# Fixing the order of all engines by a list schedule in the kernel, with a narrower chunk mask

## The chip, the cores and the metric

The kernel runs on one core of one Trainium2 chip. The metric is the time of one execution on the device in microseconds (us), median of several runs; lower is better. The core has five engines that run side by side, each through its own list of instructions in order: TensorE (PE in the profile, with weight loads shown apart as PEld), VectorE (DVE), ScalarE (ACT), GpSimd (POOL) and SyncE (SP, which here only issues DMAs). They meet through semaphores.

## The reference

Two layers follow each other. The first is attention in which every query may look only at six chunks of 32 keys. The second is an MLP with a spatial gate.

```python
# q, k, v: (B=4, H=8, S=768, D=64);  chunk = 32, 24 chunks, top_k = 6
k_min, k_max = min and max of k over each chunk                   # per dimension
ub = sum_d max(q*k_min, q*k_max)                                  # (B, H, S, 24)
ub = where(chunk of query >= chunk, ub, -1e9)
top_chunks = argsort(ub)[-6:]
scores = q @ k.T / 8, masked to the chosen chunks and to key <= query
attn = softmax(scores);  x = attn @ v                             # -> (B, S, 512)

h = relu(x @ w_in)                                                # (B, S, 1024)
u, v = h[..., :512], h[..., 512:]
v_n = (v - mean(v)) / sqrt(var(v) + 1e-6)
v_s = w_spatial @ v_n + b_spatial                                 # over the sequence
out = (u * v_s) @ w_out                                           # (B, S, 512)
```

## The kernel before

The 32 heads are worked on as 16 pairs of heads, `i = 0..15`; four pairs make one batch `b`. For each pair, k and q are transposed; the minimum and maximum of k per chunk (`kmm`) are reduced on VectorE and laid out as the operand `km`; relu(q) and relu(-q) (`rq`) times `km` give the bounds `ub`; VectorE takes the eight largest of each row and marks the chunks under the sixth. The marks are written beside q, transposed with it to the operand `a`, and the score matmul adds the penalty through the operand `kh` (k with the constant `expand` in its other half). ScalarE takes the exponential, TensorE multiplies by v, VectorE normalises, and `xT` is the transposed result. When the four pairs of a batch are done, its MLP runs: groups v, u, s, o of six tiles each.

```python
TILES = [[(0, 0, 512, 0)], [(1, 128, 512, 0)], [(2, 256, 512, 0)],      # score tiles of one head
         [(3, 384, 384, 0), (1, 640, 128, 384)], [(4, 512, 256, 0), (0, 512, 256, 256)], [(5, 640, 128, 0)]]
ps_sc = ...psum_pool(bufs=3); ps_tr = ...(bufs=1); ps_acc = ...(bufs=1); ps_ml = ...(bufs=3)

def init_masks():
    nc.gpsimd.memset(later, 0.0)                       # later: [128, 5 * 2 * 24 = 240]
    nc.gpsimd.affine_select(out=lv, in_=lv, compare_op=Alu.is_ge, fill=NEG, base=CPT,
                            channel_multiplier=1, pattern=[[CPT, NQT - 1], [0, 2], [-1, NCH]])
    # ... cut: tri, the causal mask within a tile
# --- in class Pair ---
def k_transpose(self):                                 # six PE transposes into a ps_ml tile
    for t in range(NQT):
        nc.tensor.transpose(kT[:, t * P:(t + 1) * P], self.k[:, t], identity)
def k_max(self): nc.vector.tensor_reduce(self.kmm[:, 0, :], ...kT..., op=Alu.max)
def k_min(self): nc.vector.tensor_reduce(self.kmm[:, 1, :], ...kT..., op=Alu.min, negate=True)
def k_operand(self, hi):
    copy = nc.scalar.copy if self.i < 1 else nc.vector.tensor_copy
    copy(self.kh[hi][d0:d1], self.kT[d0:d1])
def bounds(self):
    ub = self.ub = ps_tr.tile([P, 512], F32, tag="tr", name="ub")
    mm(ub[:, 0:(NQT - 1) * W], lhsT=sub_chunk, rhs=later, start=True, stop=False)        # 240 columns
    for qi in range(1, NQT):
        for m in range(2):
            mm(ub[:, (qi - 1) * W:qi * W], lhsT=self.rq[:, m, qi * P:(qi + 1) * P], rhs=self.km[:, m]..., ...)
def a_copy(self, hi):                                  # pairs 0..7; pairs 8..15 by a DMA transpose
    copy = nc.vector.tensor_copy if self.i < 2 and hi == 0 else nc.scalar.copy
    copy(self.a[:, :, hi, :], self.tr...)
def scores(self, hi, g):                               # matmul and exponential are one step
    sc = ps_sc.tile([P, 512], F32, tag="sc", name="sc")
    # ... cut: one or two matmuls, for batch 0 the causal mask by one more
    nc.scalar.activation(out=self.e[hi][...], in_=sc[:, 0:width], func=Act.Exp, scale=scale)
# ... cut: values, normalise, x_transpose
# --- the order: a table of beats, twelve to a pair ---
for i, p in enumerate(pairs):
    t0 = i * BEATS
    for hi in range(2):
        for g in range(len(TILES)):
            at(t0 + 6 * hi + g, p.scores, hi, g)
        at(t0 + 6 * hi + 6, p.values, hi, LOWER[0], True)
        # ... cut
first, count = (b + 1) * HP * BEATS + 13, HP * BEATS   # beats of the MLP of batch b
for cost, fn in steps:
    at(first + done * count // total, fn)
# ... cut: start-up steps by hand
with tc.manual_schedule(engines={mybir.EngineType.PE}):
    for beat in sorted(b for b in beats if b < 6):
        for fn, args in beats.pop(beat):
            fn(*args)
for beat in sorted(beats):
    for fn, args in beats[beat]:
        fn(*args)
```

Only TensorE's order up to beat 6 is fixed by hand; all else goes to the framework's scheduler in the order of the beats. A step may hold instructions of several engines.

Of the kernel before, what the change touches and what calls it, by code (L numbers as in the profile page):

```python
# [10 lines left out]
F32 = mybir.dt.float32  # L11
# [5 lines left out]
P = 128  # L17
# [29 lines left out]

@with_exitstack
def kernel(
# [12 lines left out]
    B, H, S, D = q.shape  # L62
# [4 lines left out]
    NQT = S // P  # L67
    NDO = DM // P
    KO = DH // P
    HP = H // 2  # L70
    NPAIR = B * HP
    CPT = P // CHUNK
    scale = 1.0 / math.sqrt(D)
    mm = nc.tensor.matmul

# [4 lines left out]
    ps_sc = ctx.enter_context(tc.psum_pool(name="ps_sc", bufs=3))  # L80
    ps_tr = ctx.enter_context(tc.psum_pool(name="ps_tr", bufs=1))
    ps_acc = ctx.enter_context(tc.psum_pool(name="ps_acc", bufs=1))
    ps_ml = ctx.enter_context(tc.psum_pool(name="ps_ml", bufs=3))

    def ml_tile():
        return ps_ml.tile([P, 512], F32, tag="mlp", name="mlp")
# [3 lines left out]

    BEATS = 12
    beats = defaultdict(list)

    def at(beat, fn, *args):
        beats[beat].append((fn, args))

    HALF = ((0, D), (D, 2 * D))


    NB = 4
    v_ring = [ring.tile([P, 4, NQT, D + 2], F16, name=f"vt{i}") for i in range(3)]
    qs_ring = [ring.tile([P, 2, NQT, 4, D], F16, name=f"qs{i}") for i in range(3)]
# [5 lines left out]
    later = cp.tile([P, (NQT - 1) * 2 * NCH], F16)  # L110
    expand = cp.tile([D, S], F16)
    eps_t = cp.tile([P, 1], F32)

    def init_identity():
        nc.vector.memset(identity, 0.0)
        nc.gpsimd.affine_select(out=identity, in_=identity, compare_op=Alu.not_equal, fill=1.0,
                                base=0, channel_multiplier=1, pattern=[[-1, P]])

    def init_ring(i):

        nc.vector.memset(qs_ring[i][:, :, :, 0:4:3, :], 0.0)

    def init_small():
        nc.vector.memset(km_ring[0], 0.0)
        nc.vector.memset(km_ring[1], 0.0)
        nc.vector.memset(eps_t, 1e-6)
        for t in v_ring:
            nc.vector.memset(t[:, :, :, D:D + 2], 1.0)

    def init_expand():  # L130

# [5 lines left out]

    def init_masks():

        nc.gpsimd.memset(later, 0.0)  # L140
        lv = later.rearrange("p (t h c) -> p t h c", h=2, c=NCH)
        nc.gpsimd.affine_select(out=lv, in_=lv, compare_op=Alu.is_ge, fill=NEG, base=CPT,
                                channel_multiplier=1, pattern=[[CPT, NQT - 1], [0, 2], [-1, NCH]])
# [4 lines left out]
    def init_kh(i):  # L148
        for hi, (d0, d1) in enumerate(HALF):
            nc.scalar.copy(kh_ring[i][hi][d0:d1, :], expand)  # L150


    W = 2 * NCH
    xT = {}
    tiles = {}

    class Pair:
        def __init__(self, i):
            self.i = i
            self.b, self.hp = divmod(i, HP)  # L160
            self.heads = [4 * (self.hp // 2) + self.hp % 2 + 2 * hi for hi in range(2)]
            self.qs = qs_ring[i // 2 % 3][:, i % 2]
            self.kh, self.km = kh_ring[i % NB], km_ring[i % 2]
            self.e = {}

        def k_transpose(self):
            if self.i < 16:
                self.kT = kT = ps_ml.tile([P, S], F16, tag="mlp", name="kTp")
                for t in range(NQT):
                    nc.tensor.transpose(kT[:, t * P:(t + 1) * P], self.k[:, t], identity)  # L170
            else:
                self.kT = sb.tile([P, S], F16, tag="kT", name="kT", bufs=3)
                nc.sync.dma_start_transpose(out=self.kT.rearrange("d (t s) -> d t s", s=P),
                                            in_=self.k.rearrange("p t h d -> p (t h d)"))

        def k_max(self):
            self.kmm = sb.tile([P, 2, NCH], F16, tag="kmm", name="kmm")
            nc.vector.tensor_reduce(self.kmm[:, 0, :], self.kT.rearrange("d (c ch) -> d c ch", ch=CHUNK),  # L178
                                    axis=AX.X, op=Alu.max)

        def k_min(self):
# [71 lines left out]
        def a_copy(self, hi):  # L253
            if self.i >= 8:
                return
# [339 lines left out]
```

The softmax here doesn't subtract the row's maximum and nothing guards it: scores larger than these inputs give would overflow.

## Time and profile before

| | |
|---|---|
| time, median of 3 runs | 208.62 us (208.17 to 208.92) |
| span of the profiled execution | 206.9 us |
| exponentials (L271, ScalarE) | 192, 96.9 us busy |
| score matmuls (L266) | 256 |
| MLP matmuls (L388) | 432 |
| product with v (L289) | 672 |
| mask matmuls (L219), 240 columns | 16 |
| software DMA queue | 12.20 MB, 89.8% of 16 engines' span |

L numbers are lines of the kernel. The busy time of an engine is the time in which an instruction of it was running; matmuls are pipelined and their ends are modelled, so a TensorE that looks busy may still have gaps between the starts of its matmuls. The chain of waits is the work that ended last, followed back from the last instruction to whatever released it. In the timeline a row is a run of like instructions of one engine: start, length, engine, line, operation, and in brackets the idle time before it with what ended it.

### The profile page before, as it was taken

The page shows a single profiled execution, that of the slowest core. Times are in us where ns is not written, and L with a number is a line of the kernel's source. Part 1 is how long each engine was busy: PE and PEld are TensorE (multiplying, and loading weights), DVE is VectorE, ACT ScalarE, POOL GpSimd, SP SyncE. Part 2 cuts the span into 40 slices and gives each one's busy share as a digit, 9 for nine tenths or more (in the row PEclk, how much of TensorE's full clock was granted, in tenths as well). Part 3 has the DMA queues.
Part 4 walks back from the last instruction along what each step waited for, and adds up shares of the span by engine and source line. Part 5 has one row for each costly group of instructions (what it writes and reads, how often), then busy time and mean ns, then how long its engine had stood idle before and what let it go on. Part 6 is the DMA issues. An engine that isn't in the chain of part 4 may idle for free.

```text
span 206.9 us, 5068 instructions
## 1 busy us (share of the span) xinstructions
PE 187.8 (91%) x1922; PEld 115.1 (56%) x1922; DVE 154.5 (75%) x454; ACT 158.1 (76%) x326; POOL 80.5 (39%) x100
## 2 busy tenths in 40 slices
PE   0368999898899999999999999999999999999992
PEld 0266776775666665656655656565555454444440
DVE  6467979989799989899797999887647456365520
ACT  4797989899998889785989996669999830666042
POOL 7997659596992463236114111111111110000000
PEclk9999999999999999999999999999999999999999
DMA  5999999999999999979998926648782124540356
GB/s 38 92 118 154 140 178 158 173 177 167 177 162 162 97 119 128 135 130 147 149 278 153 180 62 57 127 88 158 181 166 65 38 29 92 187 152 3 72 128 256
DMA packets 114424, 27.27 MB, mean 132 GB/s; under 512 B 109536, under 2 KB 110816, under 8 KB 114400
## 3 DMA queue, kind: packets, MB, share of 16 engines
q0 software_dynamic: 76544, 12.20, 89.8%
q1 hardware_dynamic: 37856, 14.75, 36.4%
q8 instruction: 15, 0.25, 0.5%
q14 instruction: 9, 0.07, 0.1%
HBM read 24.38 MB, written 6.29 MB: 148 GB/s over the span
## 4 chain that ended last, share of the span: by engine, by line
PE 69%; ACT 17%; DVE 8%; issue 2%; DMA 2%; POOL 0%; DVEq 0%; ACTq 0%; POOLq 0%
PE mlp L388 40%; PE sc L266 12%; ACT e L271 10%; PE acc L289 7%; PE kTp L170 2%; ACT a L257 2%; DVE kmm L178 2%; PE ub L222 2%; DMA k<-in_k_dram 2%; PE trm L251 2%; ACT vraw L398 1%; PE tr L205 1%; DVE vn L412 1%; DVE kmm L182 1%; ACT u L420 1%
## 5 line engine op out<-in xcount | busy, mean ns | idle before, releaser
L271 ACT ACTIVATE e<-sc 128x512 f16<-128x512 f32 x192 | 96.9, 553 | 14.8 <-PE sc L266 13.4
L266 PE MATMUL sc<-a,kh 128*128 128x512 f16 (+3 forms) x256 | 65.5, 308 | 2.1 <-ACT e L271 1.5
L388 PE MATMUL mlp<-w_in_sb,xT 128*128 128x512 f16 x192 | 53.0, 379 | 0.1
L278 POOL TENSOR_SCALAR_AFFINE_SELECT e<-e 128x768 f16<-128x768 f16 x24 | 20.9, 869 | 66.3 <-ACT e L271 66.3
L289 PEld LDWEIGHTS <-e 128*128 128x128 f16 x672 | 31.4, 97 | 17.0 <-DVE x L297 3.8
L388 PE MATMUL mlp<-vn,wsT 128*128 128x512 f16 x144 | 37.3, 379 | 0.0
L289 PE MATMUL acc<-vt,e 128*128 128x65 f16 x672 | 35.3, 193 | 0.7 <-DVE x L297 0.4
L266 PEld LDWEIGHTS <-kh 128*128 128x128 f16 x256 | 22.7, 98 | 13.3 <-issue 0.8
L437 ACT COPY o<-mlp 128x512 f32<-128x512 f32 x24 | 14.1, 586 | 19.5 <-PE mlp L388 19.1
L400 DVE BATCH_NORM_STATS2 stats<-vraw 128x6 f32<-128x512 f32 x24 | 16.6, 693 | 12.9 <-ACT vraw L398 12.5
L388 PE MATMUL mlp<-w_out_sb,gT 128*128 128x512 f16 x96 | 25.1, 379 | 0.0
L388 PEld LDWEIGHTS <-xT 128*128 128x128 f16 x192 | 17.2, 97 | 12.6 <-issue 0.4
L427 DVE SCALAR_TENSOR_TENSOR g<-mlp,b_col,u 128x512 f16<-128x512 f32 x24 | 17.9, 748 | 7.3 <-PE mlp L388 6.2
L232 DVE MAX8 max<-ub 128x8 f32<-128x8 f32 (+4 forms) x160 | 15.6, 165 | 5.1 <-PE ub L222 4.9
L388 PEld LDWEIGHTS <-wsT 128*128 128x128 f16 x144 | 12.9, 98 | 10.4
L178 DVE TENSOR_REDUCE kmm<-kTp 128x24 f16<-128x768 f16 x16 | 15.2, 948 | 3.7 <-PE kTp L170 2.7
L297 DVE TENSOR_TENSOR x<-acc,rec 128x384 f16<-128x384 f32 x32 | 17.6, 551 | 0.4
L336 POOL DMA_DIRECT2D qs<-in_q_dram x14 | 14.6, 1049 | 5.9 <-PE sc L266 5.9
L194 DVE COPY kh<-kTp 64x768 f16<-64x768 f16 x30 | 16.5, 549 | 0.5
L398 ACT ACTIVATE vraw<-mlp 128x512 f32<-128x512 f32 x24 | 14.4, 601 | 3.0 <-PE mlp L388 3.0
L420 ACT ACTIVATE u<-mlp 128x512 f16<-128x512 f32 x24 | 14.3, 598 | 1.7 <-PE mlp L388 1.5
L327 POOL DMA_DIRECT2D k<-in_k_dram x14 | 14.4, 1045 | 2.5 <-PE kTp L170 1.8
(67 smaller groups left out, 230.2 us busy)
## 6 DMA issues: line engine op xcount, KB each, us to landing
out_dram<-o SPq DMA_DIRECT2D x24, 256.0 KB, 2.3
vt<-in_v_dram POOLq DMA_DIRECT2D x8, 384.0 KB, 8.8
k<-in_k_dram POOLq DMA_DIRECT2D x14, 192.0 KB, 8.1
qs<-in_q_dram POOLq DMA_DIRECT2D x14, 192.0 KB, 7.5
ws_raw<-in_moe_w_spatial_dram POOLq DMA_DIRECT2D x6, 192.0 KB, 6.9
w_in_sb<-in_moe_w_in_dram POOLq DMA_DIRECT2D x8, 128.0 KB, 6.9
w_out_sb<-in_moe_w_out_dram POOLq DMA_DIRECT2D x4, 128.0 KB, 7.9
k<-in_k_dram POOLq DMA_DIRECT2D x4, 96.0 KB, 3.4
```

What stands on the lines that cost most here:

```text
L178: nc.vector.tensor_reduce(self.kmm[:, 0, :], self.kT.rearrange("d (c ch) -> d c ch", ch=CHUNK), axis=AX.X, op=Alu.max)
L194: copy(self.kh[hi][d0:d1], self.kT[d0:d1])
L266: mm(sc[:, col:col + n], lhsT=self.kh[hi][:, t * P:(t + 1) * P], rhs=self.a[:, q0 // P:(q0 + n) // P, hi, :], start=True, stop=not diag)
L271: nc.scalar.activation(out=self.e[hi][:, g * 512:g * 512 + width], in_=sc[:, 0:width], func=Act.Exp, scale=scale)
L278: nc.gpsimd.affine_select(out=blk, in_=blk, compare_op=Alu.is_ge, fill=0.0, base=0, channel_multiplier=-1, pattern=[[0, NQT], [1, P]])
L289: mm(self.av[:, qi, :], lhsT=self.e[hi][:, c:c + P], rhs=self.v[hi][:, t, 0:D + 1], start=first and n == 0, stop=last and n == len(blocks) ...
L297: nc.vector.tensor_tensor(self.x16[:, :, hi, :], in0=self.av[:, :, 0:D], in1=rec.to_broadcast([P, NQT, D]), op=Alu.mult)
L388: mm(st[group][:, 0:cols], lhsT=lhsT, rhs=rhs, start=(j == 0), stop=(j == n - 1))
L398: nc.scalar.activation(st["vraw"][:, ti, :], h, func=Act.Relu)
L400: nc.vector.bn_stats(stats, st["vraw"][:, ti, :])
L420: nc.scalar.activation(st["u"][:, ti, :], h, func=Act.Relu)
L427: nc.vector.scalar_tensor_tensor(g, in0=vs, scalar=b_col[:, ti:ti + 1], in1=st["u"][:, ti, :], op0=Alu.add, op1=Alu.mult)
```

## The change

The kernel brings its own scheduler. It describes every step as work of a single engine (matmul and exponential, for instance, become two steps), with a duration, the steps it depends on, the buffers it takes and frees, and a priority that is much like the beat it had. It plays these through once while the program is built, always starting the step that can start earliest and, among steps within 0.02 us, the one with the smallest priority. The kernel then emits the steps in that order, and the order holds on every engine. The aim is that no engine waits for a step that the framework's own estimates put at the wrong place. The dependencies in the model are those of data and of buffers.

The second part is the mask: for the bounds of a query tile only the four chunks of the tile itself need one, since the later ones are never looked at. So `later` shrinks to 5 x 2 x 4 = 40 columns, written by one matmul into the columns of each tile's own chunks. `PLAN` also lets the MLP of a batch begin 8 rather than 13 beats after its last pair's beats.

```diff
+def lat(a,b):
+    if a==b: return {'PE':0.0,'ACT':0.0,'DVE':0.0,'POOL':0.0,'SP':0.0}.get(a,0)
+    if b=='PE': return 0.055 if a!='DMA' else 0.135
+    if b in('ACT','DVE'): return 0.037 if a!='DMA' else 0.1
 # ... cut
+class Sim:
 # ... cut
+                tm=min(t for t,_ in lst)
+                t,o=min(((t,o) for t,o in lst if t<=tm+0.02),key=lambda x:(x[1].prio,x[1].idx))
+                if best is None or t<best[0]: best=(t,o)
 # ... cut
+            op(f'kT{i}','PE',6*mmc(128),PEL,deps=lk+['id1'],acq=[('ml',f'k{i}')],uses=[('k',g)],prio=pr(0)); kr=('ml',f'k{i}')
+        op(f'kmax{i}','DVE',km,.08,deps=[f'kT{i}'],acq=[('kmm',i)],uses=[kr],prio=pr(1))
+        op(f'kmin{i}','DVE',km,.08,deps=[f'kT{i}'],uses=[kr,('kmm',i)],prio=pr(2))
+            op(f'kop{i}{hi}',ke,(.70 if ke=='ACT' else .46) if not kd else .22,.1,deps=[f'kT{i}'],acq=[('kh',i)],uses=[kr],prio=pr((3 if hi==0 else 8)))
 # ... cut: all other steps
+                op(f'ex{i}{hi}{gg}','ACT',.493 if gg<5 else .16,.104,deps=[f'sc{i}{hi}{gg}'],acq=[('e',f'{i}{hi}')],uses=[('sc',f'{i}{hi}{gg}')],prio=t0+6*hi+gg+.1)
 # ... cut
+PLAN = {'late': 40, 'mlp_first': 8}
-    later = cp.tile([P, (NQT - 1) * 2 * NCH], F16)
+    later = cp.tile([P, (NQT - 1) * 2 * CPT], F16)
-        nc.gpsimd.affine_select(out=lv, in_=lv, compare_op=Alu.is_ge, fill=NEG, base=CPT,
-                                channel_multiplier=1, pattern=[[CPT, NQT - 1], [0, 2], [-1, NCH]])
+        nc.gpsimd.affine_select(out=lv, in_=lv, compare_op=Alu.is_ge, fill=NEG, base=0,
+                                channel_multiplier=1, pattern=[[0, NQT - 1], [0, 2], [-1, CPT]])
-            mm(ub[:, 0:(NQT - 1) * W], lhsT=sub_chunk, rhs=later, start=True, stop=False)
+            own = bass.AP(ub.tensor, ub.offset + CPT, [list(ub.ap[0]), [W + CPT, NQT - 1], [NCH, 2], [1, CPT]])
+            mm(own, lhsT=sub_chunk, rhs=later, start=True, stop=False, skip_group_check=True)
-    with tc.manual_schedule(engines={mybir.EngineType.PE}):
-        for beat in sorted(b for b in beats if b < 6):
-            for fn, args in beats.pop(beat):
-                fn(*args)
-    for beat in sorted(beats):
-        for fn, args in beats[beat]:
-            fn(*args)
+    order = build(PLAN)
+    order.run()
+    with tc.manual_schedule():
+        for o in order.emitted:
+            acts[o.name]()
```

## The prediction

> **What bounds the kernel now.** I read the page first: its busy times, the chain that ended last, and the clock row.
>
> ```profile
> span 206.9 us, 5068 instructions
> ...
> PE 187.8 (91%) x1922; PEld 115.1 (56%) x1922; DVE 154.5 (75%) x454; ACT 158.1 (76%) x326; POOL 80.5 (39%) x100
> ...
> PEclk9999999999999999999999999999999999999999
> ...
> PE 69%; ACT 17%; DVE 8%; issue 2%; DMA 2%; POOL 0%; DVEq 0%; ACTq 0%; POOLq 0%
> ```
>
> TensorE is the busiest and carries 69% of the chain, at full clock. But 17% of the chain is ScalarE and 8% VectorE: somewhere TensorE doesn't set the pace. So next the busy times by stretch (columns: window, its length, then busy us and instructions of each engine, clock, DMA share, GB/s).
>
> ```profile
> 0.00:15.00 15.00, 4.97 (x44) 3.84 (x45) 8.57 (x29) 10.86 (x15) 13.81 (x22) 1.00 1.25 80
> 15.00:55.00 40.00, 35.82 (x523) 26.94 (x522) 34.94 (x112) 36.06 (x78) 30.60 (x40) 1.00 2.26 165
> 55.00:80.00 25.00, 24.39 (x294) 16.17 (x292) 23.72 (x79) 22.38 (x48) 15.72 (x18) 1.00 2.03 136
> 80.00:160.00 80.00, 80.00 (x821) 47.84 (x820) 65.97 (x197) 67.91 (x149) 18.66 (x20) 1.00 1.06 139
> 170.00:203.00 33.00, 33.00 (x158) 14.92 (x156) 16.61 (x31) 13.98 (x25) 0.00 (x0) 1.00 0.41 114
> ```
>
> A busy TensorE here includes the modelled tail of each matmul, so I also measured it from start to start in the timeline. Back to back, a 512-column matmul takes 0.216 us (the last long piece of the chain, below: 31.53 us for 146), 384 columns 0.162, 256 0.108, 128 0.056, 65 0.030, 48 0.025. By the counts of the page that is 528 x 0.216 + 32 x 0.162 + 64 x 0.108 + 450 x 0.056 + 672 x 0.030 + 160 x 0.025 plus 16 mask matmuls of 0.102: 176 to 177 us. The first matmul starts at 5.75 and the last ends at 203.0, so TensorE lacks work for about 21 us: by the gaps between starts, 7.0 before 15 us, 10.5 between 15 and 55, 2.1 between 55 and 80, and under 2 in all the rest. The first MLP matmul starts at 55.1. From there TensorE is the bound and the end is fixed: what counts is how early it gets there, and with how much work left.
>
> The chain of waits over the start-up and at the end:
>
> ```profile
> 5.75 0.81 PE kTp L170 x6
> ...
> 6.58 0.96 DVE kmm L178
> 7.54 0.88 DVE kmm L182
> ...
> 8.50 0.79 ACT kh L194
> ...
> 9.81 0.71 ACT rq L212
> ...
> 10.57 0.56 PE ub L222 x9
> ...
> 11.15 0.93 DVE max L232 x10
> ...
> 12.10 0.42 DVE qs L237
> ...
> 16.20 1.13 ACT e L271 x2
> ```
>
> ```profile
> 171.50 31.53 PE mlp L388 x146
> 203.05 0.58 ACT o L437
> ```
>
> The start-up is a relay without slack, one engine at a time. Between 15 and 55 us ScalarE is busy 36.1 of 40 us and VectorE 34.9: the attention of the first pairs is bound by these two, and the 4 to 5 us that they lose there are what a better order can win.
>
> [...] the ScalarE copy of kTp at 8.50 starts only when VectorE's second reduction of kTp is through (8.42), though it needs nothing from it.
>
> **The change part by part.**
>
> *Mask.* The 240-column matmul becomes 40 columns.
>
> ```profile
> 63.80 0.26 PE L219 MATMUL ub<-later,sub_chunk 128*128 128x240 f16 x1
> 63.90 0.41 PE L222 MATMUL ub<-km,rq 128*128 128x48 f16 x10
> ```
>
> Its successor starts 0.10 us after it; 40 columns should take the 0.025 of the 48-column ones. 16 x 0.077 = 1.2 us of TensorE work, but some 7 of the 16 lie in the stretch where TensorE has slack; the other 9 give 0.7. The memset and select of the smaller mask on GpSimd save some tenths off the path.
>
> *Start-up.* Three things move, all against. The identity select comes between the two first k loads on GpSimd: the second is issued 0.3 us later, so the first transposes end 0.3 later. VectorE's maximum of kT, ScalarE's copy of its first half, VectorE's minimum and ScalarE's second copy now alternate, and the new program waits at each change[...]: reduction 0.95, copy 0.8, reduction 0.9, copy 0.8, then ReLU 0.65 and bounds copy 0.45. From a first reduction at 6.9 the bounds matmuls become ready at 11.6 rather than 10.5. And pair 1's minimum (0.9) and one operand copy (0.5) now stand among pair 0's maxima and its select, pair 1's two ReLU parts (0.9) before pair 0's operand copy, and pair 1's bounds before the first score matmul. The select ends at 15.0 rather than 12.5, the first exponential starts at about 17.1 rather than 15.3. Most of this is only moved: pair 1's own preparation is then done. Before, ScalarE loses 2 us around pair 0 (18.0 to 18.6, and 20 to 22); now pair 0's twelve exponentials (5.3), three operand copies of 0.7 and no gaps bring pair 1's first exponential to 24.0, against 23.4.
>
> *First four pairs.* I count ScalarE's new order: twelve exponentials take 5.25 us (ten at 0.49, two at 0.165), an operand copy 0.70, a bounds copy 0.47. Pair 1: 5.25 + 2 copies, 24.0 to 30.9 (before 31.3). Pair 2: 5.25 + 2 copies + 0.47, to 38.0 (before 39.8). Pair 3: 5.25 + 2 copies + 2 x 0.47, to 45.6 (before 47.1). In the new TensorE order the first MLP matmul follows the last score matmul of pair 4, which needs nine of pair 4's exponentials and one copy: 45.6 + 5.0 = 50.6. VectorE must by then have finished the copy that completes xT of batch 0; adding its order from pair 2's select (28.2) on gives 51.5. Hence 51.5 with neither engine ever waiting. Before, they wait 10% of this stretch. An order made from measured durations should lose less; I allow 1.5 us, a judgement: first MLP matmul at 53.0 instead of 55.1.
>
> *TensorE work left from there.* Summed over the two orders by the same durations: 143.8 us after, 144.1 before. So starting the MLP five beats earlier brings no larger reservoir; it only follows the work closer.
>
> *The MLP of batch 0.* The new order has a hole: between the last v matmul and the first u matmul stand 5.0 us of TensorE work but 6.85 us of ScalarE work (eleven wide exponentials, two narrow, a relu, an rstd, an operand copy, a bounds copy). The u tile must wait for pair 8's transposed k, which keeps a slot of the same three-deep pool until VectorE has copied its second half. There TensorE idles about 1.85 us. Before, it idles 2.0 in 55 to 80 in all; if half of those other gaps stay, the change loses 1.85 + 1.0 - 2.0 = 0.85.
>
> *The rest.* Same matmuls, and the same tail (last MLP stretch, copy, store: 3.9 us after the last matmul). I take its idle as before.
>
> Sum: 53.0 + 143.8 + 3.8 (idle before: 203.0 - 55.1 - 144.1) + 0.85 + 3.9 = 205.35 against 206.9, i.e. -1.55 us. On the median of 208.62 that is 207.1; I say 207.0.
>
> **Rivals.** *A: the order works as planned.* ScalarE and VectorE stay full from 15 to 55 us, the first MLP matmul starts at 51 and the hole closes: 203 to 204.5. For it: the windows show that the loss is there to be had. Against it: start-up is longer by the relay above, and 36 us of ScalarE work leave at most 4. *B: head-of-line blocking.* Every engine now has one fixed order, and a duration or load that is off by 0.5 us stops an engine; between 80 and 160 us TensorE shows no gap before, so there it can only get worse. VectorE's 8.1 us of work per 8.7 us of TensorE's around pair 7 leaves little slack. With 1% lost over the 150 us: 208.5 to 210. *C: loads.* The software DMA queue is 89.8% taken in the page; an order that assumes a landing too early would stall both k transposes of pairs 2 and 3, which the new order puts early. The issue order on GpSimd is almost the same, so I give it little. *D: the mask alone counts.* All else cancels: 207.9.
>
> **Range and chances.** The sum's weak terms are the 1.5 us of stalls in the head (0 to 3.5) and the steady stretch (-0.5 to +3). That spans 205.3 to 210 around 207.0; with A's chance the range is 203.8 to 210.0. Faster by 2% means under 204.45 and needs nearly all of A: 0.17. Slower by 2% means over 212.8 and needs B at several places: 0.07. The rest, 0.76, is within 2%.
>
> **What would show it.** In the new profile: mask step 0.025 us instead of 0.10; the first exponential at about 17 us and alternating VectorE and ScalarE waits on the first kT; pair 1's exponentials at about 24; the first MLP matmul near 53; a gap of TensorE of nearly 2 us before the first u matmul; then no gaps to the end, 143.8 us of work. Wrong would be: a first MLP matmul before 51.5 or after 55; idle TensorE of more than 2 us between 80 us and the end; or a start-up that isn't longer.

## The result, and the profile after

The changed kernel takes **212.21 us** (211.74 to 212.92), the kernel before, measured beside it, 208.77 us (208.17 to 209.17): ratio 1.0162, 95% interval 1.0131 to 1.0192. The prediction was 207.0 us with a range up to 210.0; the change makes the kernel 1.6% slower. Two profiles of the experiments below, the first of the narrow mask alone and that of all three moves together, fell in disturbed executions and are not read.

First the page of the changed kernel: span, busy time by engine, granted clock, and the chain that ended last.

```profile
span 210.0 us, 5059 instructions
...
PE 187.0 (89%) x1922; PEld 113.4 (54%) x1922; DVE 156.8 (75%) x454; ACT 156.2 (74%) x326; POOL 80.7 (38%) x100
...
PEclk9999999999999999999999999999999999999999
...
PE 66%; DVE 23%; ACT 5%; issue 2%; DMA 2%; POOL 1%; POOLq 0%; DVEq 0%
```

The counts of instructions on each engine are as before and the busy times nearly so. What turned over is the chain: VectorE carries 23% of it (before 8%) and ScalarE 5% (before 17%). Then the busy times by stretch, in the columns known from before:

```profile
0.00:15.00 15.00, 3.67 (x34) 2.76 (x34) 9.13 (x30) 10.58 (x16) 13.64 (x22) 1.00 1.24 79
15.00:55.00 40.00, 35.58 (x529) 27.30 (x530) 36.44 (x115) 35.07 (x75) 27.32 (x37) 1.00 2.22 155
55.00:80.00 25.00, 23.41 (x276) 15.06 (x274) 21.96 (x75) 21.38 (x46) 16.36 (x18) 1.00 1.72 136
80.00:160.00 80.00, 78.57 (x807) 46.24 (x805) 66.40 (x194) 65.70 (x145) 20.63 (x22) 1.00 1.05 143
```

From 80 to 160 us TensorE was busy 80.00 of 80 us; now 78.57. From 55 to 80 it loses another 1.0 us. Before 55 us little is won.

Measured from start to start of the matmuls:

| | before | after | predicted |
|---|---|---|---|
| first exponential | 15.3 | 17.18 | 17.1 |
| first exponential of pair 1 / 2 / 3 / 4 | 23.4 / 31.3 / 39.8 / 47.1 | 24.44 / 34.06 / 41.37 / 49.41 | 24.0 / 30.9 / 38.0 / 45.6 |
| first MLP matmul | 55.09 | 54.85 | 53.0 |
| TensorE work from there | 143.4 | 143.1 | 143.8 |
| idle TensorE from there | 4.1 | 7.5 | 4.65 |
| start of the last matmul | 202.63 | 205.50 | |

The two rows on work and idle time are counted here with the shortest steps from start to start that the traces show (0.215 us for 512 columns, 0.055 for 128, 0.029 for 65); with the durations of the prediction the kernel before had 144.1 us of work and 3.8 us of idle time there. So only the differences between the columns "before" and "after" can be set against the prediction: 0.3 us less work, as predicted, and 3.4 us more idle time, where 0.85 was predicted.

The head (all ahead of the first MLP matmul) brought 0.2 us instead of 2.1, and behind it 3.4 us of idle TensorE were added. Where they are is in the timeline of TensorE (start, length, instruction; in brackets the idle time before it and what ended it):

```profile
67.55 1.52 PE L579 MATMUL sc<-a,kh 128*128 128x512 f16 x6 [0.61 <-ACT e L588]
69.39 0.44 PE L520 MATMUL trq<-identity,qs 128*128 128x128 f16 x5 [0.31 <-ACT a L569]
71.00 1.53 PE L579 MATMUL sc<-a,kh 128*128 128x512 f16 x5 [0.32 <-ACT e L588]
...
114.09 0.19 PE L536 MATMUL ub<-later,sub_chunk 128*128 128x40 f16 x1 [0.63 <-DVE rq L530]
...
125.34 0.19 PE L536 MATMUL ub<-later,sub_chunk 128*128 128x40 f16 x1 [0.57 <-DVE rq L530]
```

The first three belong to the hole before the first u matmul (72.70): from start to start the gaps between 67.5 and 72.2 add up to 2.9 us. The last two are head-of-line blocks: bounds matmuls come up in TensorE's order before their ReLU is done, and TensorE stands still for 0.80 and 0.74 us from start to start, though MLP matmuls further down its list are ready (experiment 4 moves them ahead). Another 0.39 is lost at 95.7. Before, no gap behind 80 us is over 0.25 us except one of 0.55 at 162.5.

### The profile page after: what moved, and what is told of

Its sections match the earlier page's. It is cut to its first block, busy times and chain, and to the rows that moved or that the text cites. A ratio compares the mean times of both kernels' runs of the same rounds, so it can differ in the third digit from the quotient of the medians.

```text
span 210.0 us, 5059 instructions
## 1 busy us (share of the span) xinstructions
PE 187.0 (89%) x1922; PEld 113.4 (54%) x1922; DVE 156.8 (75%) x454; ACT 156.2 (74%) x326; POOL 80.7 (38%) x100
## 4 chain that ended last, share of the span: by engine, by line
PE 66%; DVE 23%; ACT 5%; issue 2%; DMA 2%; POOL 1%; POOLq 0%; DVEq 0%
PE mlp L676 41%; PE sc L579 11%; DVE kmm L506 7%; PE acc L605 7%; DVE kh L515 3%; DVE x L613 3%; DVE max L549 2%; ACT e L588 2%; PE ub L539 2%; PE tra L566 2%; PE kTp L490 2%; DVE rq L528 2%; DVE stats L699 2%; DMA k<-in_k_dram 2%; DVE rq L530 2%
## 5 line engine op out<-in xcount | busy, mean ns | idle before, releaser
L588 ACT ACTIVATE e<-sc 128x512 f16<-128x512 f32 x192 | 95.3, 558 | 15.3 <-PE sc L579 12.3
L676 PE MATMUL mlp<-w_in_sb,xT 128*128 128x512 f16 x192 | 52.4, 379 | 0.1
L676 PE MATMUL mlp<-vn,wsT 128*128 128x512 f16 x144 | 39.0, 379 | 0.0
L605 PE MATMUL acc<-vt,e 128*128 128x65 f16 x672 | 35.9, 193 | 1.2 <-DVE x L613 1.0
L506 DVE TENSOR_REDUCE kmm<-kTp 128x24 f16<-128x768 f16 x32 | 29.5, 948 | 7.3 <-PE kTp L490 6.4
L716 DVE SCALAR_TENSOR_TENSOR g<-mlp,b_col,u 128x512 f16<-128x512 f32 x24 | 17.9, 748 | 12.2 <-PE mlp L676 11.7
L676 PE MATMUL mlp<-w_out_sb,gT 128*128 128x512 f16 x96 | 26.9, 379 | 0.0
L549 DVE MAX8 max<-ub 128x8 f32<-128x8 f32 (+4 forms) x160 | 15.3, 165 | 1.2 <-PE ub L539 1.0
L490 PE MATMUL kTp<-identity,k 128*128 128x128 f16 x96 | 8.4, 229 | 7.0 <-DMA k<-in_k_dram 7.0
```

Of the source, the lines that this page charges most:

```text
L506: nc.vector.tensor_reduce(self.kmm[:, m, :], src, axis=AX.X, op=op, negate=(m == 1))
L549: nc.vector.max(self.max8[:, qi - 1, hi, :], self.ub[:, c0:c0 + CPT * (qi + 1)])
L588: nc.scalar.activation(out=self.e[hi][:, g * 512:g * 512 + width], in_=self.sc[hi, g][:, 0:width], func=Act.Exp, scale=scale)
L605: mm(self.av[:, qi, :], lhsT=self.e[hi][:, c:c + P], rhs=self.v[hi][:, t, 0:D + 1], start=first and n == 0, stop=last and n == len(blocks) ...
L676: mm(st[kind, ti], lhsT=lhsT, rhs=rhs, start=(j == 0), stop=(j == n - 1))
L716: nc.vector.scalar_tensor_tensor(g, in0=st["s", ti], scalar=b_col[:, ti:ti + 1], in1=st["u"][:, ti, :], op0=Alu.add, op1=Alu.mult)
```

## The experiments

Times are medians with the ratio to the kernel before and its interval; that kernel ran beside every group (208.66 to 208.87). In the names of steps the letters tell the work and the first number the pair or batch: `kT8` transposes pair 8's k, `kmax`, `kmin` and `kop` reduce and copy it, `qT` and `rq` prepare q, `ub` computes the bounds, `top` and `sel` make the selection, `aT` and `ac` the operand, `sc`, `ex`, `av` and `nm` are scores, exponentials, product with v and normalising, `x3` is the copy that completes xT of the first batch, `lq` a load of q, `wsT` a transpose of w_spatial, `u00` the first u tile.

**1. Is fixing the order the harm?** Two kernels take the same steps in the same order of the list, but leave all engines, or all but TensorE, to the framework's scheduler.

```diff
-    with tc.manual_schedule():
+    # a_free: no manual_schedule;  a_pe: tc.manual_schedule(engines={mybir.EngineType.PE})
         for o in order.emitted:
```

> The changed kernel's single-engine steps handed over in the list schedule's order, but the framework's scheduler may reorder them on all engines. Theory 1 (what costs is that the fixed order blocks engines at the head of their queues): at or under the kernel before, 207.5 to 209 us. Theory 2 (what costs is the list order itself: pair 1 pulled forward in the start-up, pair 8's k transposed before the u matmuls): the framework follows the order it is given, and the time stays at 211 to 213 us.

> The changed kernel with only TensorE's order fixed, the other engines left to the framework's scheduler. Theory 1: if the damage is done by fixed orders on ScalarE, VectorE and GpSimd, 208 to 209.5 us. Theory 2, with TensorE's order as the carrier (the hole before the first u matmul, the bounds matmuls that wait for relu(q)): 211.5 to 213 us, with the hole of nearly 3 us still there.

Measured: all free 215.93 us (1.0338, 1.0287 to 1.0390); only TensorE fixed 224.45 us (1.0750, 1.0730 to 1.0769). Giving the freedom back makes it worse, which speaks against the first theory; both times lie beyond the figures of the second. (That a fixed order need not be slower than the kernel before shows experiment 7, where the order is fixed on every engine too.) With TensorE alone fixed, the timeline has one stop of 6 us:

```profile
62.62 0.51 PE L605 MATMUL acc<-vt,e 128*128 128x65 f16 x6 [6.03 <-POOL e L594]
```

The product with v waits for the causal triangle on GpSimd. In the changed kernel GpSimd does the first two triangles of the second batch at 53.0 and 56.3; here, at 61.70 and 64.55, behind nine loads that it issues from 50.5 us on. Of the three, the order fixed on one engine alone is the slowest.

**2. The mask by itself.** `b_mask` is the kernel before with the 40-column mask (diff as in the change); `a_wide` the changed kernel with the old 240-column mask, in the same order of steps.

> The kernel before with nothing changed but the mask of 40 columns. If the mask is worth what its TensorE time says (16 x 0.077 us, of which about 0.7 us lies where TensorE is the bound), the time is 207.7 to 208.2 us, 0.3 to 0.5% under the kernel before. If the strided output of the mask matmul costs something in its own right, it is 209 us or more, and part of the slowdown is the mask's.

> The changed kernel with the old mask of 240 columns, the order of all steps kept. If the mask gives what it should in the new order too: 212.7 to 213.4 us, 0.5 to 1.2 us over the changed kernel. If the narrow mask hurts there: under 212 us.

> The kernel before with the 40-column mask once more, for a profile. If the mask matmul is itself the harm: its successor starts 0.1 us or more after it, or a new wait stands at the bounds. If the framework's rearranging is: the mask takes 0.025 us, TensorE work is 1.1 us less, and 3 to 6 us of idle TensorE appear elsewhere; 211 to 213.5 both ways.

Measured: narrow mask in the kernel before 213.14 (1.0161, 1.0091 to 1.0230) and, repeated, 211.17 us (1.0133, 1.0075 to 1.0190): slower, where the first expectation was a gain of 0.7. Wide mask in the new order 212.62 (1.0173, 1.0145 to 1.0202), the same as narrow. From the first MLP matmul to the last it took 151.26 us with the wide and 150.65 with the narrow mask, 0.6 us, about what nine masks of 0.077 come to. The matmul is harmless. What cost time in the kernel before is what the framework did with it: compared instruction by instruction, at least 64 of TensorE's 1922, 17 of VectorE's 454, 11 of ScalarE's 326 and 4 of GpSimd's 100 stand elsewhere. GpSimd's timeline near 53 us, before:

```profile
52.93 0.86 POOL L278 TENSOR_SCALAR_AFFINE_SELECT e<-e 128x768 f16<-128x768 f16 x1
53.74 1.43 POOL L343 DMA_DIRECT2D vt<-in_v_dram  x1
```

and the chain of waits with the narrow mask in it:

```profile
44.12 8.32 DMA k<-in_k_dram
...
53.34 1.41 POOL vt L345
54.75 0.06 issue
54.81 0.88 POOL e L280
55.68 0.04 issue
55.73 0.36 PE acc L291 x6
```

The v load now stands ahead of the triangle, and the chain reaches it only after a k load has landed at 52.44; TensorE waits 1.26 us for the triangle. In all TensorE has 1.2 us less work and 2.9 us more idle time. No run has the narrow mask in the order of the kernel before, so that the rearranging makes all of it is inferred.

**3. Does the longer start-up reach the end?** The start-up is moved back, by a small helper that takes steps out of the emitted order and puts them behind another.

```diff
     order.run()
+    move(['id1'], 'lk010');  move(['kmin0'], 'kmax0');  move(['kb0'], 'kop00')
+    move(['rq01'], 'rq00');  move(['kop01'], 'rq01')
+    move(['top00','top01','sel0','aT00','ac00','kT1','kmax1','sc000','sc001','qT1',
+          'kmin1','kop10','rq10','rq11','kop11'], 'ub0')
+    move(['kb1'], 'ex002');  move(['ub1','top10','top11','sel1'], 'sc010')
+    move(['aT10','aT11','ac10','kT2','kmax2'], 'sc013');  move(['kT3'], 'sc014');  move(['ac11'], 'ex013')
```

> The new order with only the start-up moved back: VectorE's maximum and minimum of the first kT stand together ahead of ScalarE's copy, pair 0's select comes before pair 1's preparation, pair 1's bounds and operand transposes go among pair 0's score matmuls, and the identity select comes after the second k load. Both theories: first exponential near 15.4 us instead of 17.2. Theory D (the start-up's delay reaches the end, as the prediction's step has it): pair 1's first exponential near 22.7, first MLP matmul 53.0 to 53.5, 210.3 to 210.9. Theory V (VectorE is the bound between 21 and 54 us and does the same work whatever the start): VectorE has not less to do before x3, so the gain shrinks to 0.5 us or less, first MLP matmul 54.2 to 54.9, 211.7 to 212.3.

Measured: 212.55 us (1.0185, 1.0158 to 1.0213), no gain at all, theory V and more. The first exponential starts at 14.56 instead of 17.18, and nothing of it is left at pair 2. VectorE's timeline there, with these moves:

```profile
21.40 0.56 DVE L569 COPY a<-tra 128x768 f16<-128x768 f16 x1 [0.55 <-PE tra L566]
22.15 1.82 DVE L506 TENSOR_REDUCE kmm<-kTp 128x24 f16<-128x768 f16 x2 [0.20 <-PE kTp L490]
```

and in the changed kernel:

```profile
17.71 0.41 DVE L554 TENSOR_TENSOR qs<-ub,max 128x240 f16<-128x240 f32 x1
20.16 0.56 DVE L569 COPY a<-tra 128x768 f16<-128x768 f16 x1 [2.05 <-PE tra L566]
21.57 1.82 DVE L506 TENSOR_REDUCE kmm<-kTp 128x24 f16<-128x768 f16 x2 [0.85 <-PE kTp L490]
```

VectorE comes to pair 2's reductions at 22.15, in the changed kernel at 21.57. From there on both are the same: it is 33.28 us to the first MLP matmul in both. In the wide mask's profile it is 33.26, in those of the next two moves 33.27 and 33.28, though the reductions start anywhere from 20.95 to 22.15. What lies between shows in the windows (third busy column VectorE, fourth ScalarE), before:

```profile
25.00:35.00 10.00, 9.45 (x147) 7.11 (x144) 8.64 (x33) 8.91 (x20) 7.42 (x11) 1.00 2.17 167
35.00:45.00 10.00, 8.97 (x135) 6.94 (x134) 9.43 (x30) 9.20 (x21) 7.79 (x11) 1.00 1.69 174
45.00:55.00 10.00, 8.38 (x138) 6.31 (x136) 8.43 (x26) 9.34 (x21) 8.13 (x10) 1.00 2.06 171
```

and after:

```profile
25.00:35.00 10.00, 8.51 (x145) 6.67 (x144) 9.80 (x38) 7.50 (x16) 6.39 (x10) 1.00 2.21 147
35.00:45.00 10.00, 8.58 (x143) 7.16 (x142) 9.84 (x28) 9.86 (x23) 5.82 (x9) 1.00 1.86 162
45.00:55.00 10.00, 8.90 (x140) 6.38 (x139) 9.82 (x29) 9.94 (x23) 7.07 (x9) 1.00 2.05 159
```

VectorE is full (9.80 to 9.84 of 10), while ScalarE starves at first (7.50). From the start of pair 2's reductions to that of the copy that completes xT it takes 31.07 us, where the kernel before took 33.04. So here the list order wins 2.0 us, as hoped.

With VectorE full from there on, what counts is when it gets pair 2's transposed k. That k has landed at 19.05, but its transposes start only at 20.95: TensorE has 93 matmuls ahead of them, and VectorE stands idle for them and for a pair 1 operand (0.85 and 2.05 us above). In the kernel before the same k lands at 18.55, 80 matmuls stand ahead of the transposes, they start at 18.85 and the reductions at 19.97. So the start-up costs 1.6 us after all, and nearly all that the list order then wins is gone. The moves of this experiment don't touch that: one of them (`kT2` behind `sc013`) puts 106 matmuls ahead of these transposes, which start 2.7 us after the landing. The experiment shows that earlier exponentials of pair 0 are worth nothing, not that the start-up is.

One thing that looks like a fault isn't: VectorE does pair 3's maximum, minimum and an operand copy before pair 2's select, for which pair 2's scores wait. The select comes 7.65 us after pair 2's first reduction (before: 5.85). But in `o_head` of experiment 7, which has the better head, it comes 8.40 us after.

**4. Are the gaps behind the head paid in full?** Each of three moves takes one of them away.

```diff
     order.run()
+    # a_hole
+    move(['rs0'], 'ex515');  move(['kop80','kop81'], 'nm50');  move(['u00.0'], 'av512');  move(['u00.2'], 'sc610')
+    move(['wsT2'], 'sc611');  move(['u01.0'], 'sc612');  move(['ua00'], 'ex612');  move(['u01.2'], 'sc613')
+    # a_ub
+    move(['ub12'], 'v14.0');  move(['ub13'], 's10.0')
+    # a_all: the start-up's, the hole's and the bounds' moves together
```

> The new order with only the neighbourhood of the first u matmul moved: the two halves of the eighth pair's operand copy come right after pair 5's normalising, so that the PSUM slot is free 1.5 us earlier; the first u matmuls stand among pair 6's scores from 70.3 us on; the rstd stands two exponentials later. Theory D (idle TensorE after the first MLP matmul is paid in full at the end): the 2.9 us of gaps between 67.5 and 72.2 shrink to about 1, and the time to 210.2 to 210.7. Theory V (pairs 6 to 8 are bound by ScalarE and VectorE): the gaps only move behind, first s matmul of batch 0 at most 0.5 us earlier, 211.8 to 212.3.

> The new order with only two bounds groups moved on TensorE: that of pair 12 behind the next v matmul and that of pair 13 behind the next s matmul, so that TensorE no longer stands still 0.80 us at 114.1 and 0.74 us at 125.3 while MLP matmuls are ready. Theory D (paid in full): both gaps under 0.2 us and 210.7 to 211.1. Rival (given back at the next wait, because the selection of pairs 12 and 13 comes later): 211.9 to 212.4, with new gaps of as much within the next 15 us.

> All three moves together. Theory D (the losses add up): 207.2 to 208.3, first MLP matmul 53.0 to 53.5, so a version as fast as the kernel before or a little faster. Theory V (the head and the middle are bound by VectorE and ScalarE, only the two bounds gaps are real): 210.3 to 211.2.

Measured: hole 212.40 us (1.0163, 1.0124 to 1.0203), bounds 211.52 (1.0143, 1.0106 to 1.0181), all together 212.17 (1.0154, 1.0120 to 1.0187). With the hole mended, the first u matmul starts at 70.89 instead of 72.70, and soon after there is a new stop:

```profile
73.81 0.50 PE L566 MATMUL tra<-identity,qs 128*128 128x128 f16 x6
75.20 0.18 PE L536 MATMUL ub<-later,sub_chunk 128*128 128x40 f16 x1 [0.89 <-ACT a L569]
75.22 0.41 PE L539 MATMUL ub<-km,rq 128*128 128x48 f16 x10
```

Bounds and transposed operand share the single buffer of `ps_tr`, and the copy that frees it comes as late as before. From the first MLP matmul to the last it is 150.79 us with the hole mended, 150.65 without: nothing won. (The two rows also show the narrow mask's 0.02 us.) The two bounds moves give 150.14: of 1.5 us of stops 0.5 is won, and new stops of 0.40 and 0.46 stand before scores at 113.4 and 124.3. The hole comes out at theory V's figure, the bounds between theory D and the rival; all together is slower than both theories had it, and where is not known. These gaps could not be taken away one at a time: what the next steps wait for came no earlier, and the wait returned a little later.

**5. Is it the plan's numbers?** The plan's durations were compared with the trace; most agree within 0.02 us, five do not. `a_cal` corrects four of them, `a_model` all five and three omissions. The omissions are read from the trace of the changed kernel: its last half-speed matmul lies at 19.4 us, its first load is issued at 1.32, and on the first kT VectorE and ScalarE never run at the same time (each of the three changes comes 0.03 to 0.04 us after the other engine has ended).

```diff
-        op(f'kb{i}',kbe,.39 if kbe=='ACT' else .47, ...
+        op(f'kb{i}',kbe,.50 if kbe=='ACT' else .52, ...
-            op(f'nm{i}{hi}','DVE',.59, ...
+            op(f'nm{i}{hi}','DVE',.69, ...
-            op(f'vs{b}{ti}','DVE',.72, ...
+            op(f'vs{b}{ti}','DVE',.83, ...
-        op(f'rs{b}','ACT',.3, ...
+        op(f'rs{b}','ACT',.45, ...
+    # only a_model: first half of the operand copy .575; all engines free from 1.3 us on;
+    half=o.occ if e=='PE' and t<19 else 0.0              # TensorE at half speed
+    if r in bank and bank[r].eng!=e: t=max(t,bank[r].end)   # VectorE and ScalarE on one PSUM tile
+    # a_model2 also: x transpose by DMA, dma=(.96,1.2) -> dma=(.96,3.7)
```

> The changed kernel's plan with only four durations corrected (normalise 0.69, statistics 0.83, bounds copy 0.50, rstd 0.45 us), nothing else. Theory M (too short durations made the order bad): 208.5 to 210. Theory G (greedy choice, and costs of other kinds, do): 211 to 214, with other gaps of the same sum.

> The same list scheduling with the same priorities, but its description of the chip corrected from the trace of the changed kernel: five durations (normalise 0.69 instead of 0.59 us, statistics 0.83 instead of 0.72, bounds copy 0.50 instead of 0.39, first half of the operand copy 0.575 instead of 0.46, rstd 0.45 instead of 0.30), TensorE at half speed until 19 us, a start 1.3 us later, and no overlap of VectorE and ScalarE on one PSUM tile. Theory M (the order is bad because the plan was made with wrong costs and without some waits): the time falls by 2.5 to 3.5 us, to 208.7 to 209.7, x3 near 49.5 and first MLP matmul near 53.3. Theory G (the greedy rule is at fault, whatever its costs): 211 to 213.

> The plan with all corrections and the landing of the x transposes by DMA set to 5.1 us, the median in the trace of the changed kernel, instead of 2.6. Against the corrected plan before it only 16 steps change place, all near 97 to 106 us: v of the second batch goes behind the output matmul of the first. If the estimate of the landing is the cause of the 3.18 us stop at 102.6: the stop falls under 1.2 us and the time to 212.5 to 214.3. If the stop has another cause: 215 to 217.

Measured: four durations 217.30 us (1.0404, 1.0386 to 1.0422); all but the DMA 215.91 (1.0317, 1.0270 to 1.0363); with the DMA 211.82 (1.0177, 1.0129 to 1.0226). Better numbers made a worse order twice, worse than either theory had it. `a_model` did help the head as far as VectorE goes (the copy that completes xT starts at 50.29 instead of 52.64), but the first MLP matmul comes 4.2 us after it instead of 2.2, at 54.47; and both plans lost 3 us at one place. TensorE in `a_cal`:

```profile
104.53 0.39 PE L676 MATMUL mlp<-w_in_sb,xT 128*128 128x512 f16 x1 [2.70 <-DMA xT<-x]
```

The transpose of x by DMA lands 7.7 us after its issue at 96.81; the plan expects 2.6. `a_model2` differs from `a_model` in 16 steps, all near this place, and is 4.1 us faster, though its transpose lands no earlier (8.0 us for 7.8): the stop falls from 3.18 us to 0.51 because the v matmuls come later in the order. In `a_cal` the stop costs more than its length: TensorE's granted clock (the third column from the end) is halved soon after it, to 0.50, for the first time since the start:

```profile
105.70:109.00 3.30, 3.30 (x20) 1.83 (x18) 2.19 (x6) 1.59 (x5) 0.86 (x1) 0.50 1.27 268
```

A 512-column matmul takes 0.427 us there instead of 0.216. Over the stretch that is 1.6 us more than at full speed; in `a_model` the same happens from 102.6 to 106.0, right after its stop, with the same cost. Stop and half speed come to 4.5 us in `a_cal`, which is 5.1 us slower than the changed kernel: otherwise its order is hardly worse. With all of it corrected the plan still gives no better order than the uncorrected one (212.21): wrong numbers explain such a stop, not the loss.

**6. Why are the transposes late?** In `a_cal` a v load and two q loads (192 KB each) are issued within 2.5 us of the x transpose. The two q loads are moved, and nothing else:

```diff
+    move(['lq70', 'lq71'], 'lv7')
```

> The plan with the four corrected durations, with the same two q loads moved from 96.9 us behind the last v load. Theory L: the x transpose issued at 96.8 lands in about 5 us instead of 7.7, the 2.86 us stop before the second batch's v at 104.5 falls to 1.5 or less, time 214.3 to 216.2. Rival: the stop stays, 216.7 to 217.6.

GpSimd's issues in `a_cal` as it was:

```profile
94.68 1.43 POOL L432 DMA_DIRECT2D vt<-in_v_dram  x1 [2.57 <-PE sc L579]
96.12 0.88 POOL L594 TENSOR_SCALAR_AFFINE_SELECT e<-e 128x768 f16<-128x768 f16 x1
96.94 2.04 POOL L425 DMA_DIRECT2D qs<-in_q_dram  x2
```

and TensorE at the same place with the q loads later:

```profile
101.58 0.39 PE L684 MATMUL mlp<-w_in_sb,xT 128*128 128x512 f16 x1 [0.65 <-DMA xT<-x]
```

Measured: 213.24 us (1.0231, 1.0191 to 1.0272), 4.1 us less than `a_cal`, more than expected. The transpose, issued at 95.94, lands 5.6 us later, and the stop shrinks from 2.86 to 0.81 us from start to start. Of the 4.6 us between the two profiles 0.9 lie before the first MLP matmul, where the orders are the same (the half speed at the start ended earlier, see the end); the other 3.7, all between 99 and 111 us, are the shorter stop and the half speed behind the long one, of which `a_cal2` shows nothing. That loads in flight delay the transposes is shown in these runs by moving only the loads (5.6 us for 7.7 here, 4.8 for 11.0 in `o_all3`).

**7. Is it the order at all?** Same steps, engines, buffers and durations. Only steps that follow one another on an engine were exchanged, and an exchange was kept when the measured durations, added up along the orders with all waits, ended no later. `o_head` exchanges only steps that start before 54 us, `o_rest` only those behind 55 us, `o_all` any; `o_all2` does so again with later landings of the DMAs allowed for, and `o_all3` is that with the two q loads of experiment 6 moved.

```diff
     order.run()
+    order.emitted = [order.ops[n] for n in ORDER]
-    # TensorE in the hole, changed:  ... kT8 wsT0 av502 wsT1 ... sc613 aT71 u00.0 wsT2 u00.2 u01.0
+    # o_rest:  ... wsT0 ... kT8 ... sc604 u00.0 ... qT8 u00.2 ... sc610 wsT1 ... aT71 wsT2 u01.0
```

> The same steps on the same engines, with an order in which only steps that started before 54 us were exchanged with neighbours of their engine, as long as adding up the measured durations along the orders gave an earlier end. Theory G (greedy order loses in head and middle alike): pair 0's first exponential 16.0, kmax of pair 2 at 19.5, x3 near 49.8, first MLP matmul 51.6, and the 3 us won there stay until the end: 209.0 to 210.0. Rival S (slack: what the head wins is waited away later, as in the three single moves): first MLP matmul earlier by 3 us but time 211 to 212.3.

> As the kernel with the exchanged head, but only steps that started after 55 us were exchanged; the head is the changed kernel's. Theory G: first MLP matmul at 54.2 to 55.2 as in the changed kernel, first s matmul 78.7 instead of 80.3, first matmul of the second batch's MLP 99.9 instead of 103.1, idle TensorE after the first MLP matmul falls from 7.5 to about 1.5 us, time 205.5 to 207.5. Rival S: gaps only change place, 210.5 to 212.3.

> Both stretches exchanged freely. Theory G: the gains add up (3 in the head, 6 behind it): first MLP matmul near 50.5, last matmul near 196.5, time 201.8 to 204.5, faster than the kernel before by 2 to 3%. Rival S or a too delicate order (a step later by 0.3 us stops all behind it): 205 to 210.

> The order searched again over the whole kernel, this time so that the sum of two ends is small: with the DMA transposes landing as fast as the plan has it, and with them (and the loads) landing 2.5 to 4.5 us later. Theory R (the freely exchanged order lost 3 to 4 us to late transposes, and room for them is to be had): first MLP matmul near 51, no stop over 0.6 us behind it, 203.3 to 205.3. Rival: order and landing can't both be had, 206 to 207.5.

> The second freely exchanged order, with only the last two q loads (2 x 192 KB, for pairs 14 and 15) moved on GpSimd from 94.0 us behind the last v load, at about 113 us. Theory L (DMA transposes land late because software loads issued just ahead are still in flight): the transpose of the operand of pair 10, issued at 96.4, lands 4 to 6 us after it instead of 11, the 2.39 us stop at 107.4 falls under 0.8, time 204.0 to 205.8. Rival (it is late by itself): 206.5 to 207.5, the stop as before.

| | us | ratio to before | first MLP matmul | from there to the last | idle in it |
|---|---|---|---|---|---|
| before | 208.77 | | 55.09 | 147.54 | 4.1 |
| after | 212.21 | 1.0131 to 1.0192 | 54.85 | 150.65 | 7.5 |
| o_head | 209.78 | 1.0032 to 1.0059 | 52.26 | 150.87 | 7.6 |
| o_rest | 208.09 | 0.9960 to 0.9985 | 55.85 | 146.60 | 3.7 |
| o_all | 206.68 | 0.9883 to 0.9938 | 51.09 | 149.44 | 5.6 |
| o_all2 | 206.90 | 0.9859 to 0.9921 | 50.87 | 150.55 | 6.6 |
| o_all3 | 206.26 | 0.9853 to 0.9910 | 51.17 | 148.19 | 4.2 |

The rows nearly add: a better head alone wins 2.4 us and keeps them, a better rest alone wins 4.1 us and takes the idle time under that of the kernel before, and `o_all` wins 5.5 of the 6.5. `o_head` is where it was expected, `o_rest` 0.6 and `o_all` 2.2 us short of it, the latter within its rival's 205 to 210. `o_all2` came out at its rival's figure: the search with later landings won nothing. Part of what is missing is late DMA transposes again (a stop of 1.09 us at 99.8 in `o_all`, of 2.39 at 107.4 in `o_all2`). With the two loads moved, the operand's transpose in `o_all3` lands 4.8 us after its issue instead of 11.0 and the second stop is gone; the profile is shorter by 2.0 us, but the median falls by only 0.6, between the two theories.

Where the head is won shows VectorE in `o_head`, at the place of experiment 3:

```profile
18.64 0.56 DVE L631 COPY a<-tra 128x768 f16<-128x768 f16 x1 [1.29 <-PE tra L628]
19.64 0.96 DVE L568 TENSOR_REDUCE kmm<-kTp 128x24 f16<-128x768 f16 x1 [0.45 <-PE kTp L552]
```

On TensorE 71 matmuls instead of 93 stand ahead of pair 2's k, and its transposes start 0.13 us after the k has landed. Of the 2.6 us by which the first MLP matmul comes earlier, 1.9 are won before these reductions, 0.25 between them and the copy that completes xT (30.82 us), 0.4 from there to the MLP. About 0.5 us of it is the half speed at the start, which ended earlier: set against `a_ub`, which has the changed kernel's head and where it ended at the same time, 2.1 us are left, 1.4 of them before the reductions. In `o_all` the first MLP matmul comes 1.0 us after the start of that copy instead of 2.2.

The page of `o_all3`, and its windows from 55 us on:

```profile
span 204.1 us, 5058 instructions
...
PE 185.6 (91%) x1922; PEld 113.4 (56%) x1922; DVE 157.3 (77%) x454; ACT 154.3 (76%) x326; POOL 80.2 (39%) x100
```

```profile
55.00:80.00 25.00, 24.11 (x282) 15.75 (x280) 23.96 (x67) 21.12 (x47) 18.20 (x20) 1.00 2.48 149
80.00:160.00 80.00, 79.80 (x816) 46.95 (x816) 65.47 (x194) 66.22 (x149) 18.68 (x20) 1.00 0.97 138
```

This version beats both: 1.2% under the kernel before, 2.8% under the changed one. The instructions are the changed kernel's; only their order differs.

The row of the hole in the diff shows how such an order gains. Three slots of `ps_ml` are shared by the transposed k, the transposes of w_spatial and the MLP tiles. The changed kernel puts two w_spatial transposes in behind pair 8's k, so the first u tile must wait for that k's slot; `o_rest` puts one of them ahead of that k and the other behind the first u tile, and the first u matmul starts 11.9 us after the first MLP matmul instead of 17.9.

## Why the prediction was wrong, point by point

- *Start-up: right in its figures, wrong in what they mean.* First exponential 17.18 (17.1 predicted), pair 1 at 24.44 (24.0), and VectorE and ScalarE take turns on the first kT: ScalarE's copies start at 7.87 and 9.69, each 0.03 us after a reduction of VectorE ends and after 1.16 and 1.02 us of waiting, and the second reduction at 8.70, after 0.86. The kernel before shows one such wait (0.98 us, until the copy at 8.50); why the two don't overlap is not shown. "Most of this is only moved" was wrong: the step watched the exponentials, whose place is worth nothing (experiment 3), and not pair 2's k, which TensorE's order now transposes 1.9 us after its landing. VectorE gets it 1.6 us later than before.
- *First four pairs: the first step that failed.* It took ScalarE for the bound (24.0 to 30.9, where its own terms give 30.65, then 38.0, 45.6), added VectorE's order from pair 2's select (28.2) to reach 51.5, and allowed 1.5 us of stalls. Pair 2's first exponential came at 34.06, 3.2 us late: VectorE is the bound, with 0.6 us of waiting in all from 21.57 to the first MLP matmul. If 28.2 is read as the select's start, the path measures so: the select is 1.0 us late (29.22); from it to the end of the copy that completes xT VectorE takes 24.0 us instead of 23.3 (seven normalising steps, each 0.10 longer than the plan had it, would make that); and from that end (53.19) to the first MLP matmul (54.85) pass 1.66 us of scores, products and transposes ahead of it in TensorE's order, among them six transposes that wait for VectorE, where the step had nothing. That is 3.35 for 1.5, or 1.85 us lost. "An order made from measured durations should lose less" was the judgement behind the 1.5, and it failed where one engine's order waits for another's, not in VectorE's own.
- *TensorE's work left: right.* It is 0.3 us less than before, as said, and the narrow mask steps by 0.02 us.
- *The hole: right in place and mechanism, too small.* 2.9 us of gaps for 1.85; net of the gaps elsewhere in 55 to 80 us, 1.2 for 0.85. ScalarE's own idle time was not in it: its rstd waits 0.59 us for the statistics at 66.
- *"The rest: idle as before": the second step that failed.* Behind 80 us TensorE idles 4.3 us where it idled 2.0. Rival B named it (head-of-line blocking, two stops of 0.80 and 0.74 at the bounds), but was given too little chance. Both stops went when the bounds were moved (experiment 4: in `a_ub` the bounds start at 113.85 and 125.25 with no idle time before them).
- *Sum.* Of the 4.65 us between the predicted span of 205.35 and the measured 210.0, 1.85 are the head, 2.55 the idle time behind it (3.4 for 0.85), and 0.25 the tail: from the start of the last matmul to the end it is 4.5 us, before 4.3.

Shown: the loss lies in the order of the steps (experiment 7), in the head and behind it, and neither in fixing an order on every engine (all kernels of experiment 7 do) nor in the mask matmul (2). Wrong costs account for a single stop (5, 6). That the greedy choice makes the rest is the reading that is left, since the plan with all corrections still gave 211.82 where exchanges gave 206 to 207. It is not shown: no run changes the priorities that the list schedule was given, or the 8 beats after which the MLP may begin. Which of its decisions cost how much stays open as well, for `o_head` moved at least 54 of TensorE's 579 steps, 25 of VectorE's 264 and 27 of ScalarE's 307, and `o_rest` 184, 59 and 74.

## What to carry to other kernels

An order from a greedy list schedule is only a starting point. Here it filled VectorE better than before, and yet the kernel was slower; correcting some of the numbers behind it made it worse by 5 and by 4 us, mostly at one late transpose, and with all of them corrected it was no better. When an engine is full, ask when it gets its first input and from whose list: VectorE's 31 us of work began when TensorE's list reached pair 2's k, 1.9 us after it had landed, and an earlier exponential changed nothing. Follow one path across the engines, not the busy time of each. Before repairing a gap, check what comes free behind it: mending the largest group of gaps here won nothing, exchanging many small things won 5.5 us, and moving two loads won 4 us in one order and 0.6 in another.

## What the runs showed that was not expected

- TensorE starts at half speed in these profiles (0.107 us per 128 columns for 0.056), and when that ends is not fixed: in the profiles of these kernels the last half-speed matmul lies between 16.4 us (before) and 21.6 us (`a_free`). It moves the time at which VectorE gets pair 2's k: in four profiles with one and the same order of the head (`a_wide`, `a_ub`, the changed kernel, `a_hole`), 17.9 us gives a first MLP matmul at 54.21, 18.0 at 54.33, 19.4 at 54.85 and 20.1 at 55.20. The clock row of the page shows full speed all the while at the start. Over these four the end of the half speed varies by 2.2 us; what sets it is not shown.
- Half speed came back behind three long stops of TensorE: those of 2.86 us in `a_cal`, 3.18 in `a_model` and 6.2 in `a_pe`, where it lasted 3.4, 3.4 and 6.8 us. With the one of 2.39 in `o_all2` it didn't. In `a_pe` it came once more, from 80.6 to 84.0, behind stops of at most 0.9, so the length of one stop doesn't tell all.
- From pair 2's reductions to the first MLP matmul, five profiles with the same order there agree within 0.02 us in 33.
- A DMA transpose takes 2.4 us (one of `gT` in the changed kernel) to 11.0 us (the operand's in `o_all2`) from issue to landing in these runs, and moving two loads out of its way took 2.1 us off one of them and 6.2 us off another.
- Two-instruction steps on VectorE take 0.10 us more than the plan has (reciprocal and product 0.69 for 0.59, the statistics 0.83 for 0.72).
